# A gated MLP's down projection for the second half of the rows in seven products of quarter matrices per block, with the sums of its weights formed by GpSimd during attention

## The chip, the cores and the metric

The kernel runs on one core of a Trainium2 chip. Five engines work side by side and meet at semaphores: TensorE (PE) multiplies matrices into PSUM, VectorE (DVE) and ScalarE (ACT) work elementwise and read PSUM, GpSimd (POOL) works elementwise between SBUF tiles, and SyncE (SP) issues most of the DMAs; GpSimd issues the others. The metric is the device time of one execution in microseconds, the median of several runs. "PEld" in a profile is the loading of a matmul's stationary operand, which overlaps the matmuls.

## The reference

A transformer block with adaptive layer norm: attention with 32 heads of width 18, then a gated MLP. S is 2048 rows, D is 576, F is 4608.

```python
mod = (_silu(c) @ w_mod).reshape(c.shape[0], 6, 1, -1)
sa, ca, ga, sb, cb, gb = (mod[:, 0], ..., mod[:, 5])
h = _layernorm(x, axis=-1) * (1 + ca) + sa
x = x + ga * _A_ref(h, A_wqkv, A_wo)
h = _layernorm(x, axis=-1) * (1 + cb) + sb
g = jnp.einsum("bsd,df->bsf", h, w_gate)
u = jnp.einsum("bsd,df->bsf", h, w_up)
x = x + gb * jnp.einsum("bsf,fd->bsd", _sigmoid(g) * u, w_down)
```

Everything is float32. The change touches the last line: `_sigmoid(g) * u` times `w_down`, the down projection.

## The kernel before

**Precision.** A float32 operand is split into a high part that the fast matmul format holds (`hi`, `hh`, `wh`) and a low rest (`lo`, `hl`, `wl`). A product is the sum of three matmuls: high x high, high x low, low x high.

**Stages.** Projections of q, k and v come first, then attention (`for u in range(UNITS)`, 32 units of 16 steps), then the MLP. The MLP goes over two halves of 1024 rows (`half` 0 and 1, "first half" and "second half" below), in each over `NB` = 18 blocks of 256 of the F columns. `seq` lists (half, block, k) with the seven `k` in the order of `ORDER` = 1, 6, 2, 7, 5, 4, 3.

**Gate and up projection.** They already use a scheme of seven products of quarters in place of eight (Winograd's form of Strassen's): the operands are cut in two along rows and along columns, and sums of quarters are multiplied. `product(st, k, acc, first)` (L1077) issues product `k` of a block: two accumulators, `v` = 0 and 1 (gate and up), of seven matmuls of 512 columns each. In the second half the sums of weights are loaded from DRAM (`w<-ws`), four products ahead (`LOOK`). VectorE adds the products together into the tiles `u2`, `u3` and `p1` (L1352, L1364, L1369, L1376, L1382), ScalarE takes the sigmoid of the gate's half (`gate`, L1090 and L1092), VectorE multiplies by the up half and ScalarE writes the high part `hh` (`gate_high`, L1098, L1100, L1102), and VectorE writes the low part `hl` (`gate_low`, L1107), called by `flush()`. So one block leaves 256 gated columns for 1024 rows, in four quarters `(f, r)`: `f` is the half of the 256 columns and `r` the half of the rows.

**Down projection.** `down(before, r, ...)` (L1114) multiplies the block before by its 256 rows of `w_down`: `before` 0 and 1 are called behind the products 6 and 7 of the next block. Of each 128 rows of output and each half of the 576 output columns, six matmuls of 288 columns (L1127: two `f`, three terms) accumulate in a PSUM tile `d` of the pool `pd`, which has three buffers, and VectorE adds the tile to `Oa` in SBUF (L1131). `w_down` was scaled by `gb` and split by GpSimd during attention: `down_parts()` loads a block (L849, which waits for a ScalarE instruction of its attention step by `paced`), multiplies, copies and subtracts (L864 to L866), and writes it to the DRAM tensor `wds` (L871). The loop of attention advances this generator every second step from step 72 on and empties it at step `FROM0` = 240, after which the generator `first_rows` uses GpSimd, starting with `load_wo` (L639 to L656). `down_weights(st)` (L1109) loads a block's `wds` in one DMA behind product 5.

**Order.** Within the MLP the order on PE, DVE and ACT is the order in which the program writes the instructions (`manual_schedule`, from `ORDERED` on); in attention it is so for PE alone. The queues of SP and GpSimd are ordered by a scheduler. Each engine takes its instructions strictly in order, so an instruction that waits holds all behind it. At the end of the first half its rows of `Oa` go to the output and `Oa` is filled from `x1d` for the second (L1135, L1137), on GpSimd's queue. The last block's `down` stands alone at the end.

## Time and profile before

| what | us |
|---|---|
| median of 3 runs | 2890.07 (2889.31 to 2890.46) |
| the profiled execution, its own time | 2886.99 |
| span in it, first to last instruction | 2885.2 |
| PE busy | 2833.0 (98%) |
| PEld busy | 1878.1 (65%) |
| DVE busy | 2212.5 (77%) |
| ACT busy | 1563.1 (54%) |
| POOL busy | 680.2 (24%) |
| share of PE in the chain that ended last | 91% |

All stages read from the same execution: attention lies between about 240 and 1590 us, the first half of the MLP between about 1590 and 2235, the second half from there to the end. An engine's busy share is an average over stages with different limits. The 1.8 us between the span and the execution's own time lie outside the first and last instruction.

A row of a timeline gives start, length, engine, line, operation, output tile<-input tiles, and how many instructions were merged; in brackets the idle time before it and what ended it. The length of merged rows runs to the end of the last one, which is longer than the distance between starts, because consecutive instructions overlap.

### The profile page before, as it was taken

What the parts mean: (1) busy time and instruction counts of PE and PEld (TensorE: products, weight loads), DVE (VectorE), ACT (ScalarE), POOL (GpSimd) and SP (SyncE); (2) the same over time, 40 slices, a digit from 0 to 9 for tenths busy, and PEclk for the clock granted to TensorE, in tenths of its full rate; (3) what the DMA queues carried; (4) which work ended last, traced back from release to release, by engine and by line L of the source; (5) the groups of instructions that cost most, each with busy time, mean ns of one, the idle gap of its engine ahead of it and who ended that gap; (6) DMA issues with size and microseconds to landing.
All of it is one profiled execution on the core that took longest, in us unless ns stands there. A gap on an engine that the chain in (4) does not pass through costs nothing.

```text
span 2885.2 us, 46301 instructions
## 1 busy us (share of the span) xinstructions
PE 2833.0 (98%) x17077; PEld 1878.1 (65%) x17077; DVE 2212.5 (77%) x4055; ACT 1563.1 (54%) x2941; POOL 680.2 (24%) x865
## 2 busy tenths in 40 slices
PE   7999999999999999999999999999999999999998
PEld 5974444444444444444443788888888888888888
DVE  7287888898899988999982878888897555555555
ACT  3216899999987778998779322333333111111111
POOL 4124305544313111562102322222221100000000
PEclk9999999999999999999999999999999999999999
DMA  5344113333312111221224866667767844544443
GB/s 170 126 153 137 56 57 135 128 128 125 118 52 77 40 48 32 96 101 51 69 69 138 292 212 227 239 219 269 282 247 288 296 165 167 169 161 161 161 168 123
DMA packets 136387, 429.27 MB, mean 149 GB/s; under 512 B 19100, under 2 KB 55968, under 8 KB 123872
## 3 DMA queue, kind: packets, MB, share of 16 engines
q1 hardware_dynamic: 119664, 344.20, 35.1%
q0 software_dynamic: 16496, 82.10, 8.1%
q8 instruction: 135, 2.21, 0.3%
q14 instruction: 92, 0.75, 0.1%
HBM read 267.77 MB, written 157.95 MB: 148 GB/s over the span
## 4 chain that ended last, share of the span: by engine, by line
PE 91%; DVE 3%; ACT 3%; DMA 1%; issue 1%; POOL 0%; SPq 0%; ACTq 0%; POOLq 0%; DVEq 0%
PE x L1081 27%; PE o L574 17%; PE d L1127 15%; PE s L472 12%; PE s L954 11%; PE s L297 4%; ACT p L958 2%; PE s L711 2%; PE s L348 2%; DVE mx L478 1%; PE s L598 1%; DVE w L1071 0%; DVE Oa L1131 0%; PE d L1266 0%; DMA wm<-in_w_mod_dram 0%
## 5 line engine op out<-in xcount | busy, mean ns | idle before, releaser
L478 DVE TENSOR_REDUCE mx<-s 128x1 f32<-128x512 f32 x1696 | 1076.9, 685 | 117.7 <-PE s L472 100.0
L958 ACT ACTIVATE p<-s 128x512 f32<-128x512 f32 x2048 | 1069.0, 610 | 140.8 <-PE s L472 67.0
L472 PE MATMUL s<-k,q 54*128 54x512 f32 x1920 | 606.0, 450 | 8.2 <-ACT p L958 1.8
L954 PE MATMUL s<-q,k 56*128 56x512 f32 x1920 | 554.5, 425 | 1.1 <-DVE mx L478 0.4
L574 PE MATMUL o<-p,vaug 128*32 128x512 f32 x4096 | 553.1, 605 | 0.4 <-ACT p L958 0.4
L1127 PE MATMUL d<-wd,hh 128*128 128x288 f32 x2304 | 460.8, 295 | 2.4 <-DVE Oa L1131 2.4
L954 PEld LDWEIGHTS s<-q,k 56*128 56x128 f32 x1920 | 264.3, 185 | 290.6 <-DVE mx L478 175.4
L472 PEld LDWEIGHTS s<-k,q 54*128 54x128 f32 x1920 | 272.6, 184 | 250.2 <-ACT p L958 151.4
L1127 PEld LDWEIGHTS d<-wd,hh 128*128 128x128 f32 x2304 | 373.4, 188 | 8.9 <-DVE Oa L1131 3.1
L1131 DVE TENSOR_TENSOR Oa<-Oa,d 128x288 f32<-128x288 f32 x576 | 256.6, 454 | 135.3 <-PE d L1127 129.4
L1081 PE MATMUL x<-k,w 128*128 128x512 f32 x1512 | 356.1, 390 | 2.4 <-ACT w L1062 2.4
L1127 PE MATMUL d<-wd,hl 128*128 128x288 f32 x1152 | 340.3, 295 | 0.0
L1081 PEld LDWEIGHTS x<-k,w 128*128 128x128 f32 x1512 | 281.6, 188 | 58.9 <-ACT w L1062 2.6
L1081 PE MATMUL x<-big,w 128*128 128x512 f32 x1008 | 237.1, 392 | 2.1 <-DVE u L1369 2.1
L1081 PE MATMUL x<-w,w 128*128 128x512 f32 x1008 | 235.9, 390 | 0.0
L1081 PEld LDWEIGHTS x<-big,w 128*128 128x128 f32 x1008 | 190.0, 189 | 42.0 <-DVE u L1369 2.5
L1127 PEld LDWEIGHTS d<-wd,hl 128*128 128x128 f32 x1152 | 216.2, 188 | 0.0
L1081 PEld LDWEIGHTS x<-w,w 128*128 128x128 f32 x1008 | 187.0, 188 | 36.9 <-DVE u L1352 0.3
L574 PEld LDWEIGHTS o<-p,vaug 128*32 128x32 f32 x4096 | 83.3, 108 | 161.6 <-issue 145.3
L1090 ACT ACTIVATE sg<-x 128x512 f32<-128x512 f32 x36 | 21.5, 598 | 300.7 <-PE x L1081 300.7
L1092 ACT ACTIVATE u<-u 128x512 f32<-128x512 f32 x72 | 45.4, 631 | 239.6 <-DVE u L1369 215.0
L1135 POOL DMA_DIRECT2D out_dram<-Oa x16 | 8.7, 542 | 601.3 <-DVE Oa L1131 601.3
(220 smaller groups left out, 2978.6 us busy)
## 6 DMA issues: line engine op xcount, KB each, us to landing
ws<-w SPq DMA_DIRECT2D x126, 640.0 KB
w<-ws SPq DMA_DIRECT2D x126, 640.0 KB
wd<-wds SPq DMA_DIRECT2D x36, 1152.0 KB
k<-kd SPq DMA_DIRECT2D x60, 360.0 KB
wds<-w POOLq DMA_DIRECT2D x18, 1152.0 KB, 4.8
k<-kd SPq DMA_DIRECT2D x60, 180.0 KB
w<-in_B_w_down_dram POOLq DMA_DIRECT2D x18, 576.0 KB, 4.3
q<-qd SPq DMA_DIRECT2D x64, 144.0 KB
```

The costliest lines, as they stand in the source:

```text
L297: nc.tensor.matmul(acc, w, hT[:, t, cols], start=n == 0, stop=n == len(ts_) - 1)
L348: nc.tensor.matmul(acc[:, 0:HALF], hT[:, k, rows], w, start=n == 0, stop=n == len(ts_) - 1,)
L472: nc.tensor.matmul(sp, qs[rows, qt * P : (qt + 1) * P], ks[rows, at * 512 : (at + 1) * 512], start=True, stop=True,)
L478: nc.vector.tensor_reduce(to, sp, axis=AX.X, op=ALU.max)
L574: nc.tensor.matmul(acc[32 * j : 32 * j + 32, :], vaug[:, kt, (2 * p + h) * VW : (2 * p + h) * VW + 32], probs[2 * c + h], start=kt == 0, s ...
L711: nc.tensor.matmul(acc[:, :HALF], a, w, start=i == 0, stop=i == len(ts_) - 1)
L954: nc.tensor.matmul(sT, ks[rows, kcols], qs[rows, c * 512 : (c + 1) * 512], start=True, stop=True)
L958: state["exp"] = nc.scalar.activation(pr, sT, AF.Exp, scale=SCALE)
L1081: nc.tensor.matmul(acc[v], w[:, v, a, :], X[s][:, b, :], start=first and n == 0, stop=n == 6, skip_group_check=not first,)
L1092: nc.scalar.activation(t[:, 0:512], t[:, 0:512], AF.Sigmoid)
L1127: nc.tensor.matmul(acc[:, :HALF], a[:, f, rows], w[:, f, cols], start=n == 0, stop=n == 5)
L1131: nc.vector.tensor_add(Oa[:, t, cols], Oa[:, t, cols], acc[:, :HALF])
```

## The change

In the second half, the down projection of the blocks 0 to 15 (`SEVENS` = 16) is also done in seven products. With A the gated block (quarters a11, a12 for the upper 512 rows, a21, a22 for the lower) and B the block of `w_down` (quarters of 128 rows x 288 columns), the products are those of a11, a12, a22 and the sums s1 = a21 + a22, s2 = s1 - a11, s3 = a11 - a21, S4 = a12 - s2 with quarters of B or sums of them.

- **Weights.** In attention GpSimd forms four sums of quarters per block for 16 blocks, splits them like the rest and writes them to a second DRAM tensor, `wtd`. The generator is advanced in three steps of four instead of one of two. The next block's load is issued later in a block than before.
- **The second half's loop.** For blocks 1 to 16 the loop has a branch of its own: `sevenths(j, b - 1, tiles)` issues product `j` of the block before (`TURNS` says which `j` goes with which `k`) in four tiles of three matmuls of 288 columns, two tiles behind each half `v` of `product`. VectorE adds each tile to `Oa`, or to one of four collecting tiles `G1`, `G5`, `G6`, `G7` in SBUF, which are used by more than one quarter of the output.
- **Sums of A.** `sums_of(before)` forms s1, s2, S4 and s3 on VectorE at product 1, ScalarE writes the high parts (`high`) and VectorE the low parts (`low`) later.
- **Loads.** `load_columns` loads quarters of B and their sums (288 columns each, high and low) one per product on SP's queue, a product after the last use of the quarter that they replace.
- **Joining.** During the products of the last block, `joined(n)` adds the collecting tiles to each other and to `Oa`, in eight VectorE instructions of 4 x 288 columns.

Blocks 16 and 17 keep the old `down`.

```diff
--- before.py
+++ after.py
@@ -54,6 +54,8 @@
+SEVENS = NB - 2
+TURNS = {1: 1, 6: 2, 2: 4, 7: 3, 5: 5, 4: 7, 3: 6}
...
+    wtd = dram.tile([SEVENS, P, 4 * D], F32R, name="wtd")
...
-            for i in range(4):
-                cols = slice(i * HALF, (i + 1) * HALF)
-                nc.gpsimd.tensor_mul(raw[:, cols], raw[:, cols], gb_b[:, i % 2 * HALF : (i % 2 + 1) * HALF])
-                nc.gpsimd.tensor_copy(hi[:, cols], raw[:, cols])
-                nc.gpsimd.tensor_sub(lo[:, cols], raw[:, cols], hi[:, cols].bitcast(F32))
-                if i == 1 and b + 1 < NB:
-                    ahead = load(b + 1)
-                if i < 3:
+            quads = [slice(i * HALF, (i + 1) * HALF) for i in range(4)]
+            b11, b12, b21, b22 = (raw[:, q] for q in quads)
+
+            def split(i):
+                nc.gpsimd.tensor_copy(hi[:, quads[i]], raw[:, quads[i]])
+                nc.gpsimd.tensor_sub(lo[:, quads[i]], raw[:, quads[i]], hi[:, quads[i]].bitcast(F32))
+
+            for i, q in enumerate(quads):
+                nc.gpsimd.tensor_mul(raw[:, q], raw[:, q], gb_b[:, i % 2 * HALF : (i % 2 + 1) * HALF])
+                if i == 2:
                     yield
+            if b < SEVENS:
+                two = [temp([P, 2048], F32R) for _ in range(2)]
+                (t1, t2), (t3, t4) = ([x[:, (2 + i) * HALF : (3 + i) * HALF].bitcast(F32) for i in range(2)] for x in two)
+                nc.gpsimd.tensor_sub(t1, b12, b11)
+                nc.gpsimd.tensor_sub(t3, b22, b12)
+                yield
+                nc.gpsimd.tensor_sub(t2, b22, t1)
+                nc.gpsimd.tensor_sub(t4, t2, b21)
+            if b + 1 < NB:
+                ahead = load(b + 1)
+            yield
+            split(0)
+            split(1)
+            yield
+            split(2)
+            split(3)
             nc.gpsimd.dma_start(wds[b].bitcast(F32), t[:, 0 : 4 * D].bitcast(F32))
             yield
+            if b < SEVENS:
+                for i, x in enumerate(two):
+                    for k in range(2):
+                        to, part = x[:, k * HALF : (k + 1) * HALF], x[:, (2 + k) * HALF : (3 + k) * HALF]
+                        nc.gpsimd.tensor_copy(to, part.bitcast(F32))
+                        nc.gpsimd.tensor_sub(part, part.bitcast(F32), to.bitcast(F32))
+                    nc.gpsimd.dma_start(
+                        wtd[b, :, 2 * D * i : 2 * D * (i + 1)].bitcast(F32), x[:, 0 : 2 * D].bitcast(F32)
+                    )
+                    yield
 
     def last_rows_project():
         for t in range(8, NT):
...
-            if 4 * NT + 8 <= step < FROM0 and step % 2 == 0:
+            if 4 * NT + 8 <= step < FROM0 and step % 4 != 3:
...
-    def product(st, k, acc, first):
+    def product(st, k, acc, first, halves=(0, 1)):
         s, w = ORDER.index(k), st["w", k]
-        for v in range(2):
+        for v in halves:
...
+        st["t", f, r] = t
+        if st["half"] and st["b"] < SEVENS and (f, r) == (0, 1):
+            return None
...
+    late = {}
+
+    def second_half():
+
+        rawst.close()
+        pool = ctx.enter_context(tc.tile_pool(name="late", bufs=1, side="right"))
+        late["G"] = {k: pool.tile([P, 4, HALF], F32, name=f"G{k}") for k in (1, 5, 6, 7)}
+        late["wt"] = pool.tile([P, 2, 2, 2, HALF], F32R, name="wt")
+        late["S4"] = pool.tile([P, 512], F32, name="S4")
+        late["hx"] = pool.tile([P, 3, 512], F32R, name="hx")
+        late["lx"] = pool.tile([P, 3, 512], F32R, name="lx")
+
...
+    def sevenths(j, b, tiles):
+
+        (h, l), w = rows_of(j), columns_of(j)
+        for t in tiles:
+            rows = slice(t * P, (t + 1) * P)
+            acc = pd.tile([P, 512], F32, name="d")[:, 0:HALF]
+            for n, (a, k) in enumerate(((h, 0), (h, 1), (l, 0))):
+                nc.tensor.matmul(acc, a[:, rows], w[:, k, :], start=n == 0, stop=n == 2)
+            if j in late["G"]:
+                to = late["G"][j][:, t, :]
+                if b == 0:
+                    nc.vector.tensor_copy(to, acc)
+                else:
+                    nc.vector.tensor_add(to, to, acc)
+            elif j == 4:
+                to = Oa[:, 4 + t, 0:HALF]
+                nc.vector.tensor_sub(to, to, acc)
+            else:
+                to = Oa[:, t, 0:HALF] if j == 2 else Oa[:, t, HALF:D]
+                nc.vector.tensor_add(to, to, acc)
+
+    def high(j, t):
+        nc.scalar.copy(rows_of(j)[0], t)
+        late["t", j] = t
+
+    def low(j):
+        h, l = rows_of(j)
+        nc.vector.tensor_sub(l, late.pop(("t", j)), h.bitcast(F32))
+
+    def sums_of(st):
+
+        a11, a12, a21, a22 = st["t", 0, 0], st["t", 1, 0], st["t", 0, 1], st["t", 1, 1]
+        s1, s2, s3 = (
+            sums.tile([P, 2, 3, P], F32, name=f"S{k}").rearrange("p v t c -> p (v t c)")[:, 0:512] for k in (1, 2, 3)
+        )
+        nc.vector.tensor_add(s1, a21, a22)
+        nc.vector.tensor_sub(s2, s1, a11)
+        high(5, s1)
+        high(6, s2)
+        yield
+        nc.vector.tensor_sub(late["S4"], a12, s2)
+        nc.vector.tensor_sub(s3, a11, a21)
+        high(3, late["S4"])
+        high(7, s3)
+        yield
+
+    def joined(n):
+
+        G = late["G"]
+        r0, r1 = Oa[:, 0:4, :], Oa[:, 4:8, :]
+        pairs = (
+            (G[6], G[1]), (r0[:, :, 0:HALF], G[1]), (G[7], G[6]), (r0[:, :, HALF:D], G[6]), (r1[:, :, 0:HALF], G[7]),
+            (r1[:, :, HALF:D], G[7]), (r0[:, :, HALF:D], G[5]), (r1[:, :, HALF:D], G[5]),
+        )
+        to, a = pairs[n]
+        nc.vector.tensor_add(to, to, a)
+
...
+        sevens = hf == 1 and 0 < b <= SEVENS
+        if sevens:
+            if at or b > 1:
+                load_columns(b if at else b - 1, TURNS[seq[n - 1][2]])
+            if b == 1 and k in (1, 6, 2, 7):
+                load_columns(0, {1: 3, 6: 5, 2: 7, 7: 6}[k])
+            if k == 1:
+                made = sums_of(before)
+                next(made)
+                st["a"], first = banks(), True
+                acc, to, by = st["a"], None, None
+            elif k == 6:
+                st["b_"], first = banks(), True
+                st["u2"] = ep.tile([P, 1024], F32, name="u2")
+                acc, to, by = st["b_"], st["u2"], st["p1"]
+            elif k == 2:
+                acc, first, to = st["a"], False, None
+                for r in range(2):
+                    st["hh", r], st["hl", r] = late["hh", r], late["hl", r]
+            elif k == 7:
+                st["u3"] = ep.tile([P, 1024], F32, name="u3")
+                acc, first, to, by = st["b_"], False, st["u3"], st["p1"]
+            elif k == 5:
+                st["c"], first = banks(), True
+                acc, to, by = st["c"], st["u3"], st["u3"]
+            elif k == 4:
+                acc, first, to, by = st["b_"], False, st["p1"], st["p1"]
+            else:
+                acc, first, to, by = st["c"], False, st["u2"], st["u2"]
+            f, r = {2: (0, 0), 5: (1, 1), 4: (1, 0), 3: (0, 1)}.get(k, (None, None))
+            for v in range(2):
+                product(st, k, acc, first, (v,))
+                if to is not None:
+                    nc.vector.tensor_add(half(to, v), acc[v], half(by, v))
+                if v == 0 and f is not None:
+                    t = gate(st, to)
+                sevenths(TURNS[k], b - 1, (2 * v, 2 * v + 1))
+                if v == 0:
+                    if k == 1:
+                        next(made)
+                        st["p1"] = ep.tile([P, 1024], F32, name="p1")
+                        nc.scalar.copy(half(st["p1"], 0), acc[0])
+                    elif k == 6:
+                        low(3)
+                    elif k == 2:
+                        low(5)
+                    elif k in (7, 4, 3):
+                        flush()
+                elif k == 1:
+                    nc.scalar.copy(half(st["p1"], 1), acc[1])
+            if f is not None:
+                got = gate_high(st, t, f, r)
+                if got:
+                    behind.append(got)
+            if k in (2, 7):
+                low({2: 6, 7: 7}[k])
+            if k == 3:
+                before = st
+                st["wd"] = late["wd"][:, 0], late["wd"][:, 1]
+            continue
...
+            got = gate_high(st, *kept)
+            if got:
+                behind.append(got)
+        if hf and not b and k in (4, 3):
+            load_columns(0, {4: 2, 3: 4}[k])
+        if hf and b == NB - 1:
+            for i in {1: (0, 1), 2: (2, 3), 5: (4,), 4: (5, 6), 3: (7,)}.get(k, ()):
+                joined(i)
```

Three places show how the change moves instructions. First PE, inside a block of the second half (x: an accumulator of the gate and up projection; k_ and w_: parts of the MLP's input; d: the down projection's PSUM tile; wd, wt: its weights). Before, the products 1 and 6 and the first tile of the `down` behind them:

```order
L1081 MATMUL x<-k_20118,w 128x512 x14
L1081 MATMUL x<-k_20578,w 128x512 x14
L1127 MATMUL d<-wd,hh_31562 128x288 x2
L1127 MATMUL d<-wd,hl_31563 128x288
L1127 MATMUL d<-wd,hh_31562 128x288 x2
L1127 MATMUL d<-wd,hl_31563 128x288
```

and after, the second half of product 2, the two tiles behind it, and the first half of product 7:

```order
L1113 MATMUL x<-w_20984,w 128x512 x7
L1195 MATMUL d<-wt,hh_27565 128x288 x2
L1195 MATMUL d<-wt,hl_27566 128x288
L1195 MATMUL d<-wt,hh_27565 128x288 x2
L1195 MATMUL d<-wt,hl_27566 128x288
L1113 MATMUL x<-w_20986,w 128x512 x7
```

A run of 28 matmuls of 512 columns and then 48 of 288 columns has become an alternation of 7 and 6; a tile `d` now ends after three matmuls instead of six.

Second DVE, at the seam between two of those blocks, product 3 of one (`u_...` is its `u2`) and product 1 and the first part of 6 of the next. Before:

```order
L1382 TENSOR_TENSOR u_31763<-x,u_31763 128x512 x2
L1100 TENSOR_TENSOR u_31763<-u_31763 128x512
L1107 TENSOR_TENSOR hl_31849<-u_31763,hh_31848 128x512
L1352 TENSOR_TENSOR u_32047<-x,p_32026 128x512 x2
L1131 TENSOR_TENSOR Oa<-Oa,d 128x288 x8
```

and after (G_...: collecting tiles; S_...: the sums of A; sg, u and p: the block's gated quarters):

```order
L1508 TENSOR_TENSOR u_32134<-x,u_32134 128x512
L1201 TENSOR_TENSOR G_27448<-G_27448,d 128x288 x2
L1132 TENSOR_TENSOR u_32134<-u_32134 128x512
L1223 TENSOR_TENSOR S_32389<-u_32134,u_32218 128x512
L1224 TENSOR_TENSOR S_32390<-S_32389,sg 128x512
L1201 TENSOR_TENSOR G_27446<-G_27446,d 128x288 x2
L1228 TENSOR_TENSOR S_27451<-p_32109,S_32390 128x512
L1229 TENSOR_TENSOR S_32391<-sg,u_32134 128x512
L1201 TENSOR_TENSOR G_27446<-G_27446,d 128x288 x2
L1508 TENSOR_TENSOR u_32444<-x,p_32419 128x512
L1207 TENSOR_TENSOR Oa<-Oa,d 128x288 x2
```

Between the last gating product (L1132) and the next block's first addition (L1508) there stood one low part (L1107); now there are four sums and four additions of tiles `d`.

Third DVE in the last block, products 4 and 3. Before:

```order
L1376 TENSOR_TENSOR p_32026<-x,p_32026 128x512 x2
L1100 TENSOR_TENSOR p_32026<-p_32026 128x512
L1107 TENSOR_TENSOR hl_32131<-p_32026,hh_32130 128x512
L1382 TENSOR_TENSOR u_32047<-x,u_32047 128x512 x2
L1131 TENSOR_TENSOR Oa<-Oa,d 128x288 x2
L1100 TENSOR_TENSOR u_32047<-u_32047 128x512
L1131 TENSOR_TENSOR Oa<-Oa,d 128x288 x2
```

and after:

```order
L1580 TENSOR_TENSOR p_32713<-x,p_32713 128x512 x2
L1132 TENSOR_TENSOR p_32713<-p_32713 128x512
L1243 TENSOR_TENSOR Oa<-Oa,G_27449 128x4x288
L1243 TENSOR_TENSOR Oa<-Oa,G_27447 128x4x288
L1142 TENSOR_TENSOR hl_27564<-p_32713,hh_27563 128x512
L1586 TENSOR_TENSOR u_32737<-x,u_32737 128x512 x2
L1243 TENSOR_TENSOR Oa<-Oa,G_27447 128x4x288
L1267 TENSOR_TENSOR Oa<-Oa,d 128x288 x2
L1132 TENSOR_TENSOR u_32737<-u_32737 128x512
L1267 TENSOR_TENSOR Oa<-Oa,d 128x288 x2
```

Two joining additions (L1243) now stand in front of the low part that the last `down` reads (L1142), and a third in front of the first addition of that `down` (L1267).

46 lines of the change are left out of this document (40 added, 6 removed).

## The prediction

> **What bounds the kernel now.** I read the page first, then the busy times by stage, then the chain of waits in order of time through the last block.
>
> ```profile
> PE 91%; DVE 3%; ACT 3%; DMA 1%; issue 1%; POOL 0%; SPq 0%; ACTq 0%; POOLq 0%; DVEq 0%
> L1131 DVE TENSOR_TENSOR Oa<-Oa,d 128x288 f32<-128x288 f32 x576 | 256.6, 454 | 135.3 <-PE d L1127 129.4
> 350.00:400.00 50.00, 49.65 (x330) 20.23 (x326) 44.89 (x85) 47.19 (x96) 2.68 (x4) 1.00 0.11 32
> 500.00:550.00 50.00, 49.65 (x331) 20.59 (x332) 44.78 (x85) 47.38 (x95) 21.90 (x36) 1.00 0.34 115
> 2600.00:2650.00 50.00, 50.00 (x282) 44.66 (x281) 27.65 (x49) 7.38 (x13) 0.00 (x0) 1.00 0.51 169
> ```
>
> A row of the stages holds sum, PE, PEld, DVE, ACT and POOL (instructions in brackets), clock, DMA share, GB/s. In the second half (last row) PE is never idle at full clock, DVE is busy 27.65 of 50 us, POOL not at all, and VectorE waits for PE: 129.4 us before its additions of `d`. There a matmul less is its time less, as long as VectorE keeps up. In attention PE, DVE and ACT are all near full; GpSimd has room.
>
> ```profile
> 2835.80 6.36 PE d L1127 x48
> 2842.16 6.36 PE x L1081 x28
> 2848.52 6.36 PE d L1127 x48
> 2854.89 9.53 PE x L1081 x42
> 2864.42 7.97 PE d L1127 x60
> ```
>
> The chain gives the matmuls' true distances, without the overlap that single rows hide: 6.36 / 48 = 0.1325 us for 288 columns and 6.36 / 28 = 0.227 us for 512, and no gap where one kind follows the other. A block is 98 x 0.227 + 96 x 0.1325 = 35.0 us.
>
> **The change part by part.** *Matmuls.* `down` has 2 x 4 x 2 tiles of six, 96 per block; the sevenths 7 x 4 tiles of three, 84. Sixteen blocks save 192 x 0.1325 = **25.4 us**, and a block takes 98 x 0.227 + 84 x 0.1325 = 33.4 us. Switching 28 times instead of four between the two kinds costs nothing by the rows above. [...]
>
> *VectorE in the loop.* It loses nothing and gains, per block, 12 additions of tiles, 4 sums and 3 low parts.
>
> ```profile
> L1100 DVE TENSOR_TENSOR p<-p x36: 676/692/695, 1618.2 to 2862.3; 128x512 f32<-128x512 f32 x36
> 2863.71 0.69 DVE L1107 TENSOR_TENSOR hl<-p,hh 128x512 fp32r<-128x512 f32 x1 [0.69 <-ACT hh L1102]
> 2864.32 1.28 DVE L1382 TENSOR_TENSOR u<-x,u 128x512 f32<-128x512 f32 x2
> ```
>
> With 25 instructions of 512 columns at 0.69 us and 28 of 288 at 0.454, a block needs 30.0 us of its 33.4 (before: 18 and 16, 19.7 of 35.0); the starts 2863.71 and 2864.32 show that independent instructions follow after 0.61, so the true load is lower. In a half of a product (PE: 7 x 0.227 + 6 x 0.1325 = 2.39 us) it has at most one addition of 512, two of 288 and one more of 512: 2.29. The exception is the seam of the second order fence: from the last half of product 3 through the first of product 1 it has six of 512 and four of 288, 5.96 us against 4.77. So it falls 1.2 us behind, more where the gate's multiplication must wait for the addition before it. PE feels that only when a buffer of `d` is wanted again. Laying the rows out with the full 0.69 and 0.454 plus 0.05 for each semaphore, the tightest buffer is free 0.3 us before PE needs it; with 0.61 there is over 1 us. I take **0**; if this cover is gone, PE waits once per block, some 0.5 us, 8 in all, and that is my upper bound.
>
> *Loads.*
>
> ```profile
> w<-ws SPq DMA_DIRECT2D x126, 640.0 KB
> wd<-wds SPq DMA_DIRECT2D x36, 1152.0 KB
> ```
>
> Per block seven loads of 288 KB replace the one of 1152 KB, beside seven of 640, so SP moves 6.65 MB instead of 5.77. By the last stage row, 169 GB/s at a share of 0.51, full use would be near 330 GB/s; 6.65 MB in 33.4 us is 199. A quarter is wanted six products after its load is issued, 29 us. Each of these loads waits only for the product just finished, so the next `w<-ws` behind it in SP's queue is not held: **0**.
>
> *GpSimd in attention.*
>
> ```profile
> 428.62 0.79 POOL L849 DMA_DIRECT2D w<-in_B_w_down_dram  x1 [13.44 <-ACT p L958]
> 563.14 0.71 POOL L849 DMA_DIRECT2D w<-in_B_w_down_dram  x1 [7.05 <-ACT p L958]
> 567.77 1.56 POOL L864 TENSOR_TENSOR w<-w,gb_b 128x288 f32<-128x288 f32 x2 [3.91 <-DMA w<-in_B_w_down_dram]
> 569.28 0.78 POOL L865 CAST w<-w 128x288 fp32r<-128x288 f32 x2
> 575.67 0.59 POOL L871 DMA_DIRECT2D wds<-w  x1 [0.30 <-POOL w L866]
> 774.61 0.59 POOL L871 DMA_DIRECT2D wds<-w  x1 [0.30 <-POOL w L866]
> 849.30 0.61 POOL L639 DMA_DIRECT2D t<-in_A_wo_dram  x1 [34.58 <-ACT p L958]
> 896.10 0.81 POOL L617 TENSOR_TENSOR Oa<-oT,rec 128x144 f32<-128x144 f32 x2 [4.27 <-ACT oT L613]
> L678 PEld LDWEIGHTS s<-ident,Oa x32: 138/140/145, 904.1 to 1075.0; 128*128 128x128 f32 x32
> ```
>
> A block takes 563.14 to 576.26, 13.1 us, with its load's landing. Added are eight two-input instructions of 0.78, four copies of 0.39 and two DMA issues of 0.59: 9.0, with a share of L617 22.6 us. From the first load (step 72) to `load_wo` (step 240) a step lasts (849.30 - 428.62) / 168 = 2.50 us; seven calls in three of four steps are 23.4 us. So GpSimd keeps pace and ends near 428.6 + 122 x 4/3 x 2.50 = 836 instead of 775, before 849. Does a busier GpSimd slow the others? The two stage rows of attention, at 2.68 and 21.90 us of POOL, have the same 85 DVE, 96 and 95 ACT and 330 and 331 PE instructions. **0**, and below nothing is excluded because no work leaves attention.
>
> *The joins.* A join has 4 x 288 = 1152 columns: 0.454 + 864 x (0.692 - 0.454) / 224 = 1.37 us. In the last block they stand between instructions that feed the last `down`.
>
> ```profile
> 2858.90 0.69 DVE L1100 TENSOR_TENSOR u<-u 128x512 f32<-128x512 f32 x1
> 2860.33 0.69 DVE L1107 TENSOR_TENSOR hl<-u,hh 128x512 fp32r<-128x512 f32 x1 [0.74 <-ACT hh L1102]
> 2862.33 0.69 DVE L1100 TENSOR_TENSOR p<-p 128x512 f32<-128x512 f32 x1
> 2864.25 0.42 PE L1127 MATMUL d<-wd,hh 128*128 128x288 f32 x2
> ```
>
> Product 5's join fills VectorE's wait of 0.74 and makes the rest 0.5 us late. The two of product 4 come between the multiplication (2862.33 + 0.5) and the low part that began at 2863.71: it now ends near 2866.7. PE wants it for the sixth matmul of the first tile, at 2864.25 + 5 x 0.1325 = 2864.9: 1.8 us of wait. Then product 3's two additions and the last join delay the first tile's addition to about 2869.6, while PE has its three buffers full at 2868.4: 1.2 more. Product 2's two joins make the `down` behind product 7 wait 0.2. Together **3.2 us**; 0 if I have a position wrong, 5.5 if the last four joins were all exposed.
>
> *The start of the second half.*
>
> ```profile
> 2281.22 0.55 POOL L1137 DMA_DIRECT2D Oa<-x1d  x1 [2.27 <-DMA out_dram<-Oa]
> DMA to landing us min/median/max: 4.1/4.1/4.1
> 2260.00:2270.00 10.00, 10.00 (x48) 8.36 (x47) 5.98 (x10) 2.51 (x4) 1.62 (x3) 1.00 0.91 301
> ```
>
> The last tile of `Oa` lands at 2285.3. Before, it was added to behind product 7; now product 2 of block 1 does it, near 2284.6, and eight loads of 288 KB in place of one of 1152, 1.2 MB more, come into a stretch with a DMA share of 0.91 at 301 GB/s: up to 4 us later. VectorE may stand 1 to 4 us, half of which its buffers hide: **1 us**, bounds 0 and 3.
>
> The sum: 25.4 - 3.2 - 1.0 = 21.2 us less. Span 2864.0, profiled execution 2865.8; the median of the runs shown was 3.1 above the profiled execution, so 2890.07 - 21.2 = **2868.9 us**.
>
> **The rivals.**
>
> *VectorE becomes the bound* (slower). For: 53 instructions per block in strict order, 90% by durations. It decides from 35.0 us per block. If a tile's addition cost as much as one of 512 columns (the nearest dearer row), 53 x 0.69 = 36.6 us, 16 x (36.6 - 35.0) = 26 us slower, with the joins 2919. Against: the 0.454 has 576 instances between 0.440 and 0.456. [...] Chance 0.07.
>
> *GpSimd falls behind in attention.* A block of x us makes `load_wo` 16 (x - 23.4) late; the 13 us before 849, the 4.3 before 896.10 and some 7 until PE reads `Oa` at 904.1 absorb 24, so it decides from 24.9. At 26 it gives back 18 us: 2887; at 28, 50: 2919. For: 22.6 is close, and more instructions now wait on GpSimd's own results. Chance 0.05, about half on each side of no change.
>
> *The steady loop leaks at the seams*: 8 to 15 us back, 2876 to 2884. Chance 0.11. *Joins and start are hidden*: 2864.6. Chance 0.08. Anything that I do not see, slower: 0.03. That the matmuls are not saved is excluded by the order of PE: 192 fewer.
>
> **How the numbers follow.** The forecast has 0.66, with a range of its own of 2865 to 2876. The range to 2863 and 2883 takes in the hidden joins and the leaks, by the upper bounds 25.4 - 5.5 - 3 - 8 = 9 less, 2881. About 0.2%, 5.8 us, can be told from no change: faster 0.66 + 0.08 + 0.11 = 0.85, same 0.03, slower 0.12.
>
> **What would show it.** Blocks of the second half 33.4 us apart; PE 50 of 50 there with DVE near 40 to 44; PE rows of 7 and 6 without gaps; POOL done with `wtd` before 849 and the same instruction counts in attention; waits of PE for VectorE of about 3 us in the last 20. Wrong: PE waiting for VectorE in every block, or `load_wo` late.

## The result, and the profile after

The changed kernel took 2885.48 us (median of 11 runs, 2879.64 to 2894.37), the kernel before 2891.87 (11 runs, 2888.45 to 2893.95): a ratio of 0.9982, 95% interval 0.997 to 0.9993. That is 0.18% faster, hardly to be told from no change, and outside the predicted 2863 to 2883. Here and below a ratio rests on all runs of both kernels, and can differ by up to 0.0009 from that of the medians. The runs of the changed kernel spread over 15 us, those of the kernel before over 5.5.

The profiled execution of the changed kernel is the fastest of its eleven, 2879.64. Its page begins so, and the chain that ended last no longer is almost all PE:

```profile
span 2877.8 us, 46834 instructions
PE 83%; POOL 6%; DVE 4%; issue 3%; ACT 2%; DMA 1%; SPq 0%; POOLq 0%; ACTq 0%; DVEq 0%
```

GpSimd had 0% of that chain before and has 6% now. To place the difference I cut the span at three events: the first exponential of attention, the first product of the MLP, and the last product. A row of a line's instructions gives shortest, median and longest duration in ns, and the starts of the first and of the last. The exponentials, the products with operand `k` (the first product) and with `big` (the last), before:

```profile
L958 ACT ACTIVATE p<-s x2048: 570/603/716, 238.5 to 1585.3; 128x512 f32<-128x512 f32 x187
L1081 PE MATMUL x<-k,w x1512: 387/389/481, 1590.8 to 2857.7; 128*128 128x512 f32 x189
L1081 PE MATMUL x<-big,w x1008: 387/389/632, 1606.9 to 2864.0; 128*128 128x512 f32 x168
```

and after:

```profile
L989 ACT ACTIVATE p<-s x2048: 570/603/716, 242.8 to 1600.7; 128x512 f32<-128x512 f32 x187
L1113 PE MATMUL x<-k,w x1512: 387/389/632, 1606.2 to 2850.6; 128*128 128x512 f32 x189
L1113 PE MATMUL x<-big,w x1008: 387/389/504, 1623.7 to 2856.9; 128*128 128x512 f32 x168
```

Attention, from the first exponential to the first product, went from 1352.3 to 1363.4 us; the MLP, from the first to the last product, from 1273.2 to 1250.7; the tail from 21.2 to 20.9. The MLP won 22.5 us, attention lost 11.1, and 4.3 were lost ahead of attention. (The tail ends with the last output stores.)

The steady loop of the second half is as predicted. First its row of the stages (sum, PE, PEld, DVE, ACT, POOL, clock, DMA share, GB/s), then three steps of the chain, with no gap between the kinds of matmul:

```profile
2600.00:2650.00 50.00, 50.00 (x273) 43.91 (x272) 39.48 (x80) 10.32 (x17) 0.00 (x0) 1.00 0.59 193
```

```profile
2598.05 0.80 PE d L1195 x6
2598.85 1.62 PE x L1113 x7
2600.47 0.80 PE d L1195 x6
```

The loss in attention sits in few places. Ten-microsecond rows of the changed kernel:

```profile
690.00:700.00 10.00, 7.60 (x43) 2.74 (x42) 5.91 (x11) 6.67 (x14) 10.00 (x18) 0.83 0.48 147
700.00:710.00 10.00, 10.00 (x72) 4.26 (x68) 8.59 (x17) 9.09 (x18) 6.56 (x11) 1.00 0.73 271
810.00:820.00 10.00, 6.55 (x41) 2.96 (x41) 7.10 (x14) 5.57 (x11) 9.98 (x18) 0.96 0.40 122
820.00:830.00 10.00, 9.32 (x50) 3.52 (x51) 4.81 (x10) 7.71 (x16) 5.33 (x10) 0.70 0.90 326
```

An undisturbed row (the second) has 72 matmuls; the others have 43, 41 and 50. PE is idle for 2.4 and 3.5 us, and behind each gap it runs at a lower granted clock (0.57 from 696 to 700, 0.50 from 820 to 826). Over all 135 such rows from 240 to 1590 us, PE's missing busy time rose from 13.1 to 20.8 us, and the clock that was not granted (10 us times what the clock lacks of 1.00, summed) from 2.1 to 8.5 us. A part of this is only the first row, 240 to 250, as attention began 4.3 us later. The three disturbed rows alone make 6.5 us of idle time and 5.1 us of clock, together about the 11.1 us that attention lost.

The waits of 430 to 900 us (engine, line, what for; total, times, longest) and the timeline around 690 say who was late. "POOL w L873 <- DMA w" is GpSimd waiting for a load of `w_down` to land, that is, for its data to arrive:

```profile
POOL w L873 <- DMA w<-in_B_w_down_dram: 106.9, 18, 11.8
POOL w L852 <- ACT p L989: 13.4, 1, 13.4
ACT oT L591 <- POOL Oa L620: 6.8, 2, 4.3
PE o L577 <- ACT oT L591: 6.5, 2, 4.1
```

```profile
652.38 0.73 POOL L852 DMA_DIRECT2D w<-in_B_w_down_dram  x1
664.90 3.09 POOL L873 TENSOR_TENSOR w<-w,gb_b 128x288 f32<-128x288 f32 x4 [11.79 <-DMA w<-in_B_w_down_dram]
688.13 3.10 POOL L873 TENSOR_TENSOR w<-w,gb_b 128x288 f32<-128x288 f32 x4 [5.18 <-DMA w<-in_B_w_down_dram]
693.83 0.81 POOL L620 TENSOR_TENSOR Oa<-oT,rec 128x144 f32<-128x144 f32 x2
694.67 0.59 ACT L591 COPY oT<-o 128x512 f32<-128x512 f32 x1 [2.57 <-POOL Oa L620]
695.31 1.07 PE L577 MATMUL o<-p,vaug 128*32 128x512 f32 x8 [2.40 <-ACT oT L591]
```

Line 620 (617 before) is attention's own work on GpSimd: it takes the last pair of heads out of `oT`. It stands in GpSimd's queue among the instructions of `down_parts`, here behind a multiplication that waited 5.18 us for its load, after one that had waited 11.79. `oT` has one buffer, so ScalarE may not copy the next pair's accumulator `o` into it before line 620 has read it; `o` is not free until that copy, and TensorE waits to write it. GpSimd's pacing wait (line 852 on ScalarE: a load may be issued only once the exponential of its step is done), 106.1 us in 17 waits before, is left in one wait of 13.4 us, ahead of the first load. Between the blocks GpSimd has no reserve left.

### The profile page after: what moved, and what is told of

Read it like the earlier page. It is cut to its first block, busy times and chain, and to the rows that moved or that the text cites. A ratio compares the mean times of both kernels' runs of the same rounds, so it can differ in the third digit from the quotient of the medians.

```text
span 2877.8 us, 46834 instructions
## 1 busy us (share of the span) xinstructions
PE 2820.3 (98%) x16885; PEld 1855.6 (64%) x16885; DVE 2336.0 (81%) x4367; ACT 1591.6 (55%) x2989; POOL 821.3 (29%) x1089
## 4 chain that ended last, share of the span: by engine, by line
PE 83%; POOL 6%; DVE 4%; issue 3%; ACT 2%; DMA 1%; SPq 0%; POOLq 0%; ACTq 0%; DVEq 0%
PE x L1113 26%; PE o L577 14%; PE s L475 10%; PE s L985 10%; PE d L1263 8%; PE d L1195 6%; PE s L300 4%; PE s L714 2%; PE s L351 2%; ACT p L989 2%; POOL w L870 1%; POOL t L899 1%; DVE mx L481 1%; POOL w L873 1%; PE s L601 1%
## 5 line engine op out<-in xcount | busy, mean ns | idle before, releaser
L1113 PE MATMUL x<-k,w 128*128 128x512 f32 x1512 | 369.7, 392 | 2.4 <-ACT w L1094 2.4
L1263 PE MATMUL d<-wd,hh 128*128 128x288 f32 x1280 | 256.7, 295 | 3.8 <-DVE Oa L1267 3.7
L1113 PE MATMUL x<-w,w 128*128 128x512 f32 x1008 | 245.1, 391 | 0.0
L1113 PE MATMUL x<-big,w 128*128 128x512 f32 x1008 | 244.3, 391 | 0.0
L1263 PEld LDWEIGHTS d<-wd,hh 128*128 128x128 f32 x1280 | 207.2, 188 | 8.7 <-DVE Oa L1267 5.1
L1263 PE MATMUL d<-wd,hl 128*128 128x288 f32 x640 | 189.1, 295 | 1.6 <-DVE hl L1142 1.6
L1267 DVE TENSOR_TENSOR Oa<-Oa,d 128x288 f32<-128x288 f32 x320 | 139.9, 453 | 55.6 <-PE d L1263 51.7
L1094 ACT CAST w<-S 128x768 fp32r<-128x768 f32 x72 | 60.1, 835 | 134.9 <-POOL S L1072 133.4
```

The lines of the kernel that those rows point to most:

```text
L1094: nc.scalar.copy(w[:, :, 0:3, :], src)
L1113: nc.tensor.matmul(acc[v], w[:, v, a, :], X[s][:, b, :], start=first and n == 0, stop=n == 6, skip_group_check=not first,)
L1263: nc.tensor.matmul(acc[:, :HALF], a[:, f, rows], w[:, f, cols], start=n == 0, stop=n == 5)
L1267: nc.vector.tensor_add(Oa[:, t, cols], Oa[:, t, cols], acc[:, :HALF])
```

## The experiments

Each kernel of an experiment ran beside the kernel before on the same chip. The stretches of the profiles, cut as above, are each of one execution:

| kernel | ratio to before (95%) | first exp at | attention | first to last product | tail |
|---|---|---|---|---|---|
| before | | 238.5 | 1352.3 | 1273.2 | 21.2 |
| changed | 0.9982 (0.997 to 0.9993) | 242.8 | 1363.4 | 1250.7 | 20.9 |
| after_again | 0.9974 (0.9963 to 0.9985) | 242.2 | 1362.2 | 1254.6 | 20.9 |
| second_alone | 0.9948 (0.9936 to 0.9961) | 239.9 | 1355.5 | 1251.2 | 24.1 |
| attention_alone | 1.0035 (1.0023 to 1.0048) | 241.0 | 1365.2 | 1273.0 | 17.9 |
| sums_no_stores | 1.0005 (0.9996 to 1.0014) | 243.4 | 1354.5 | 1272.5 | 21.2 |
| before_two | 1.0000 (0.9991 to 1.0009) | 242.4 | 1351.8 | 1273.0 | 21.2 |
| oT_two | 0.9951 (0.9939 to 0.9964) | 243.0 | 1362.2 | 1251.1 | 20.9 |
| oT_rec_two | 0.9932 (0.9921 to 0.9944) | 243.0 | 1352.2 | 1253.1 | 20.9 |
| load_on_SP | 0.9959 (0.9945 to 0.9972) | 243.9 | 1359.4 | 1252.0 | 24.0 |
| both_mended | 0.9960 (0.9948 to 0.9971) | 242.2 | 1359.1 | 1250.4 | 23.9 |
| joins_sooner | 0.9950 (0.9938 to 0.9961) | 239.0 | 1355.2 | 1252.8 | 22.3 |
| rec_two_joins | 0.9946 (0.9930 to 0.9962) | 243.3 | 1362.0 | 1252.1 | 19.4 |
| stores_on_SP | 1.0149 (1.0133 to 1.0164) | 243.0 | 1417.7 | 1260.4 | 22.8 |
| late_rows | 0.9926 (0.9913 to 0.9938) | 243.5 | 1352.5 | 1251.3 | 19.3 |

**The two halves of the change apart.** second_alone has the old `down_parts` and its old pace. It leaves the sums out: the second half reads plain quarters where the sums should be, with the same matmuls and the same number of bytes. Besides the old `down_parts`, its edit is this:

```diff
-            kept = wtd[b].rearrange("p (a l i d) -> p a l i d", a=2, l=2, i=2)
+            kept = wds[b].rearrange("p (a l i d) -> p a l i d", a=2, l=2, i=2)
-            if 4 * NT + 8 <= step < FROM0 and step % 4 != 3:
+            if 4 * NT + 8 <= step < FROM0 and step % 2 == 0:
```

> Leaves out the quarter sums of w_down: attention does GpSimd's old work, and the second half reads plain quarters in their place (same bytes from memory, same instructions). Theory (the gain of the second half is there in full, the loss sits in attention): about 21 us under before, ratio 0.992 to 0.993; first matmul of the first half of the MLP at about 1591 us as before, clock as before. Rival (the second half itself costs more in some executions): a spread as wide as the change's 15 us and a ratio near 0.998. Rival (the shift of 4.3 us ahead of attention is part of the change's second half, by its buffers): the first exp of attention at about 243 us instead of 238.5.

attention_alone keeps the new `down_parts`, while the second half's loop is the old one (`USED` = 0 in place of `SEVENS` there; one line of several):

```diff
-        sevens = hf == 1 and 0 < b <= SEVENS
+        sevens = hf == 1 and 0 < b <= USED
```

> Sums and their stores are made, but the second half works as before and doesn't read them. Theory: 11 to 16 us over before, ratio 1.004 to 1.0055, all of it between 450 and 900 us, with two or three idle stretches of TensorE of 2 to 4 us behind oT, each with a granted clock of 0.7 to 0.9 in the 10 us after it. Rival (GpSimd's extra work takes memory or engine time evenly): no idle stretch, but exps in each 50 us fewer by one or two. Rival (the loss needs the second half): ratio 1.000.

Measured: 2872.5 against 2889.64 for the first, 2900.37 for the second. The MLP's gain stands alone, 22.0 us between first and last product, and attention's loss stands alone, 12.9 us, with idle stretches at 690 (6.86 us busy of 10) and 810 (4.62). By their ratios the two halves, 0.52% faster and 0.35% slower, make 0.17% faster together; the whole change is 0.18% faster. Both ratios missed their ranges. That of attention_alone, 1.0035, is a little under 1.004. That of second_alone is 0.9948 where 0.992 to 0.993 was expected: its attention, though the work is the old one, was 3.2 us longer than in the profile of before, and its tail 2.9. One cause in attention is a drop of the clock that the section on the hardware shows; the tail's is open. The first exponential came between 238.5 and 243.9 us in all profiles, at 242.4 in before_two, which has no part of the change: the 4.3 us ahead of attention are a spread of executions.

**The changed kernel again.**

> The changed kernel once more, beside the others on one chip. Theory (GpSimd late, ACT then TensorE held at oT): the same two idle stretches of TensorE near 690 and 810 us, TensorE's busy time short of the 240 to 1590 us stretch by 18 to 22 us, a clock dip behind each; ratio 0.997 to 0.9995. Rival (the stretches of the first profile were a chance of that one execution): they are gone or elsewhere, and the time is near 2874 us.

2881.7 against 2889.7. The stretch at 690 us returned (7.34 us busy of 10, then a clock of 0.55 from 700 on); the one at 810 did not, and a smaller one came at 530, where ScalarE does not wait for GpSimd (TensorE waits 1.0 us for a load of `q`). So one of the two expected stretches came, ScalarE waited for `oT` once, 2.8 us, and attention still lost 9.9 us. The place varies; the loss was nearly the same.

**Whose wait it is.** oT_two gives every second pair of heads of the first half of attention a buffer of its own, and oT_rec_two doubles the small tile `rec` as well, which line 620 reads too:

```diff
-            oT = epool.tile([P, 512], F32, name="oT")
+            other = p % 2 and half == 0 and 2 < p
+            oT = bgp.tile([P, 512], F32, name="oU") if other else epool.tile([P, 512], F32, name="oT")
-        rec = epool.tile([P, 4, 4], F32, name="rec")
+        rec = epool.tile([P, 4, 4], F32, name="rec", bufs=2)
```

> Every second pair of heads of the first half of attention puts oT into a buffer of its own, so that ACT's copy doesn't wait for GpSimd's last use. Theory: GpSimd stays as late as in the change (last wds store at about 855 us, landing waits near 105 us), but ACT's wait on GpSimd for oT and the idle stretches of TensorE are gone: about 10 us under the change, ratio 0.994 to 0.995. Rival (GpSimd's lateness itself passes on to w_o and the first rows): ratio stays at 0.998 with new waits behind 865 us.

> As oT_two, and the small tile rec has two buffers as well, since with oT doubled VectorE waited 7.6 us for GpSimd at rec and TensorE 6.8 us behind it. Theory: no wait of TensorE, ACT or VectorE on GpSimd between 430 and 900 us, no 10 us stretch there under 8.5 us of TensorE, though GpSimd's landing waits stay above 100 us; 2 to 5 us under oT_two, ratio 0.993 to 0.9945. Rival (GpSimd's lateness shows at its next user): a new wait of 5 us or more on GpSimd, ratio as oT_two (0.995).

oT_two took 2874.36 against 2889.64. Its profiled execution is the slowest of its five, 2879.04. In it ScalarE's wait for `oT` on GpSimd was gone, and the next tile read by line 620 (621 in these kernels) took its place:

```profile
POOL w L874 <- DMA w<-in_B_w_down_dram: 113.9, 18, 12.4
DVE rec L606 <- POOL Oa L621: 7.6, 1, 7.6
PE s L986 <- ACT oT L617: 6.8, 1, 6.8
```

VectorE stood 7.6 us at `rec`, and TensorE 6.8 behind it. With `rec` doubled too, oT_rec_two took 2870.65 against 2889.7 (2868.87 to 2871.53), and its attention 1352.2 us, what it took before. GpSimd is as late as ever, or later:

```profile
POOL w L874 <- DMA w<-in_B_w_down_dram: 117.3, 18, 13.3
L893 POOL DMA_DIRECT2D wds<-w x18: 578/578/608, 449.5 to 865.8; - x18
```

So in this execution lateness by itself cost nothing; in the changed kernel the single buffers passed it on. The control is the same edit in the kernel before:

> The kernel before with oT and rec in two buffers and nothing else. Theory: before has no wait of ACT on GpSimd for oT, so the buffers are worth nothing there: ratio 0.9995 to 1.0005. Rival (the buffers are a gain of their own, and the change lost less in attention than it seems): ratio 0.996 to 0.998.

2890.16 against 2889.69, a ratio of 1.0000: the buffers are no gain of their own.

**Why GpSimd is late.** sums_no_stores is attention_alone without the two stores of the sums:

```diff
-                    nc.gpsimd.dma_start(
-                        wtd[b, :, 2 * D * i : 2 * D * (i + 1)].bitcast(F32), x[:, 0 : 2 * D].bitcast(F32)
-                    )
```

> attention_alone without the two stores of the quarter sums: GpSimd makes the sums, splits them, and nothing carries them out (the second half doesn't read them). Theory (the stores delay the next block's load, and that delay is what makes GpSimd late): landing waits fall from 107.8 us to under 75, GpSimd's block to about 21 us of work and then the pace, no wait of ACT on oT, ratio 0.9995 to 1.0005. Rival (the GpSimd work alone is too long): landing waits fall, but the wait of ACT on oT and the idle stretches stay, ratio 1.002 to 1.004. Rival (the load lands late without the stores as well): landing waits near 100 us.

2892.09 against 2890.53, where attention_alone had lost 10.7 us: without the stores the loss is gone. The mechanism in the expectation was only a part of it. The waits for the load fell only from 107.8 to 94.2 us:

```profile
POOL w L874 <- DMA w<-in_B_w_down_dram: 94.2, 18, 11.0
POOL w L853 <- ACT p L987: 28.2, 7, 13.4
L893 POOL DMA_DIRECT2D wds<-w x18: 593/593/611, 449.7 to 834.3; - x18
```

The larger part of the gain is the time that GpSimd itself no longer spends on issuing these stores. A row of the changed kernel shows one, with the wait for GpSimd's own last result ahead of it:

```profile
651.79 0.60 POOL L900 DMA_DIRECT2D wtd<-t  x1 [0.30 <-POOL t L899]
```

Thirty-two issues of about 0.57 us and sixteen waits of 0.30 make 23 us; with the 13.6 of landing, less 14.7 more of pacing (28.2 in place of 13.5), 22 us are removed; from the first store of `wds` to the last it is 384.6 us instead of 406.5 (449.7 to 834.3, and 447.5 to 854.0).

The 94.2 us that remain are not the same wait 18 times. In the changed kernel 14 of the 18 waits for the load last 3.6 to 6.5 us and four last 8.6 to 11.8. Without the stores of the sums 14 last 2.9 to 4.7 us, 3.7 in the mean, as before the change, and four still last 10.6 to 11.0. What the four have in common is attention's own loads of q and k, eight on SP's queue every 40 us, 1.5 MB together. Here are the first and the last of one group in the changed kernel, on both sides of the load issued at 652.38 that was waited for 11.79 us:

```profile
648.28 0.79 SPq L440 DMA_DIRECT2D q<-qd  x1
653.86 0.98 SPq L448 DMA_DIRECT2D k<-kd  x1
```

In these two profiles all eight long waits are for a load issued during such a group or within 2 us of its end, and no load issued at another time was waited for that long. In the kernel before, the pacing kept the loads clear of the groups. Every second load was issued just ahead of one, here by 0.36 us; this one was waited for 3.49 us, and no wait for a load in that kernel exceeds 5.7:

```profile
642.77 0.71 POOL L849 DMA_DIRECT2D w<-in_B_w_down_dram  x1 [7.07 <-ACT p L958]
643.13 0.78 SPq L437 DMA_DIRECT2D q<-qd  x1
```

So the stores of the sums lengthen the usual wait by about 1.1 us, some 15 us in all, and the long waits come with the loads of q and k. That rests on the times alone; no run moves those loads.

Two kernels moved DMAs to SP's queue, one the load and one the stores:

```diff
-            paced(nc.gpsimd.dma_start(
+            paced(nc.sync.dma_start(
                 t[:, 2 * D : 4 * D].bitcast(F32).rearrange("p (t d) -> p t d", d=D),
```

> The load of w_down's next block goes into SP's queue and no longer stands behind the three stores in GpSimd's. Theory: GpSimd's waits for that load fall from 106.9 us to under 50, its block to about 19 us of work ahead of the pace, no wait of ACT on GpSimd for oT, first matmul of the MLP at about 1595 us, time 2868 to 2874 (ratio about 0.993). Rival (stores and loads share the transport, whatever the queue): landing waits stay near 100 us and the time at 0.998. Rival (SP's queue then holds q, k and mrows loads back behind this load): new waits of TensorE or VectorE on q or mrows, and a time above the change's.

```diff
-            nc.gpsimd.dma_start(wds[b].bitcast(F32), t[:, 0 : 4 * D].bitcast(F32))
+            nc.sync.dma_start(wds[b].bitcast(F32), t[:, 0 : 4 * D].bitcast(F32))
-                    nc.gpsimd.dma_start(
+                    nc.sync.dma_start(
                         wtd[b, :, 2 * D * i : 2 * D * (i + 1)].bitcast(F32), x[:, 0 : 2 * D].bitcast(F32)
```

> The changed kernel (single buffers) with the three stores of a block in SP's queue instead of GpSimd's; the load stays in GpSimd's. Theory (the load lands late because it stands behind the stores in one queue): GpSimd's landing waits fall from 106.9 us to about the 64 to 67 us of before, the block from 24.6 to about 21 us, the wait of ACT on oT is gone; ratio 0.993 to 0.995. Rival (they share the transport): the waits stay over 95 us. Rival (SP's queue, full of stores that wait for GpSimd, holds q and mrows back): TensorE or VectorE waits on DMA, ratio over 0.998.

load_on_SP took 2878.55 against 2889.64, slower than the expected 2868 to 2874. GpSimd was on time (last `wds` store at 834.5) and ScalarE's wait for `oT` gone; 79.9 us of waiting for the load remained instead of under 50, a part of it pace, as SP's queue held the load 153.2 us for the step's exponential. But a stretch of 6.94 us busy of 10 came at 1430 us, far behind `down_parts`, where TensorE waits for the row tile of `project_o`. One near there is in the profiles of all three kernels with the load on SP and in no other; why is open. stores_on_SP failed by its second rival, 2935.22 against 2889.69. SP takes its queue in order and stood 201.6 us at stores whose data GpSimd had not made, ahead of the loads that TensorE needed:

```profile
SPq L892 <- POOL w L870: 201.6, 18, 29.0
POOL w L873 <- DMA w<-in_B_w_down_dram: 97.6, 18, 11.3
PE s L985 <- DMA q<-mrows: 43.2, 12, 10.3
```

Its second row is worth keeping: with no store in its own queue the load was still waited for 97.6 us. So standing behind the stores in one queue is not, or not alone, what delays it.

**Combinations.**

> oT and rec in two buffers and the load of w_down on SP's queue. Theory: each alone already takes the idle stretches away, so the two together are no faster than the better one, ratio 0.993 to 0.995, and equal to second_alone (0.9948) within its interval. Rival (each takes away a part of its own): ratio under 0.9925.

2878.4 against 2889.7, a ratio of 0.9960, slower than oT_rec_two alone and outside the expected range, with the stretch at 1430 us again: here the load is better left in GpSimd's queue.

```diff
-            for i in {1: (0, 1), 2: (2, 3), 5: (4,), 4: (5, 6), 3: (7,)}.get(k, ()):
+            for i in {1: (0, 1, 2), 2: (3, 4, 5), 5: (6, 7)}.get(k, ()):
```

> both_mended with the eight joins at products 1, 2 and 5 of the last block instead of 1, 2, 5, 4 and 3. Theory: the waits of TensorE on VectorE in the last two products (1.6 us for the low part, 0.8 us for a d buffer) go, and nothing else moves: 2 to 2.4 us less between the last product's end and the end of the span. Rival (joins in product 5 hold the gate and the high part back): a wait of TensorE on VectorE for hh or hl of 1 us or more.

> oT_rec_two with the joins sooner, the load left in GpSimd's queue. Theory: the idle stretch at 1430 us, which came with the load on SP's queue, isn't there, and the tail loses 2 to 3 us: 2867 to 2869 against 2889.7, ratio 0.992 to 0.993, the best of all. Rival (the tail is set by the last stores, not by VectorE): ratio as oT_rec_two, 0.9932.

joins_sooner took 2875.5, within both_mended's interval; its tail was 1.6 us shorter where 2 to 2.4 were expected. rec_two_joins took 2874.89 against 2889.69, and its six runs reach from 2864.88 to 2880.34: neither the 2867 to 2869 nor the best of all. Its profile shows attention 9.7 us longer than before, at the place that the prediction had feared. GpSimd waited 12.64 us for one load, finished `wds` at 873.40, and its preparation of `w_o` came too late for `project_o`:

```profile
873.40 0.58 POOL L893 DMA_DIRECT2D wds<-w  x1 [0.30 <-POOL w L871]
DVE t L688 <- POOL we L657: 7.1, 1, 7.1
PE s L475 <- DVE t L688: 5.9, 1, 5.9
```

late_rows puts six more steps of attention between that preparation and its first use:

```diff
         weights.extend((wo_h, wo_l, we))
-        for _ in range(4):
+        for _ in range(10):
             yield
```

> rec_two_joins with the first row tile's projection six steps (about 15 us) further behind w_o's preparation, since in rec_two_joins' profile GpSimd ended the weights at 873 us and the last part of w_o held VectorE 7.1 us and TensorE 5.9 us at 910 us. Theory (what is left of GpSimd's lateness shows there, in some executions): no wait behind w_o's tiles, no idle stretch at 910 us, the spread of the runs narrows from 15 us to about 5; 2867 to 2870, ratio 0.992 to 0.993. Rival (the spread comes from elsewhere, the clock dips ahead of 250 and at 1600 us): spread and median as in rec_two_joins, 0.9946.

2868.39 against 2890.53 (2867.86 to 2874.27), ratio 0.9926, the lowest of all, though its interval and that of oT_rec_two overlap. It is 22.1 us under its kernel before, where the change was 6.4 under its own. In its profile nothing waits at `w_o`, `oT` or `rec`, with GpSimd's last `wds` store at 858.1. That the spread narrowed from 15.5 to 6.4 us rests on five runs. The sooner joins bring little of it: the tail is 1.6 us shorter than in oT_rec_two, but TensorE waits 1.3 us for VectorE at 2834 instead.

## Why the prediction was wrong, step by step

- **Matmuls, VectorE, loads of the second half: right in kind, the saving put too high.** The same instruction in two successive blocks, after the change (L1223, the first sum of A) and before it (L1352, the first addition of product 1):

```profile
2353.03 0.69 DVE L1223 TENSOR_TENSOR S<-u,u 128x512 f32<-128x512 f32 x1
2386.62 0.69 DVE L1223 TENSOR_TENSOR S<-u,u 128x512 f32<-128x512 f32 x1
2344.87 0.69 DVE L1352 TENSOR_TENSOR u<-x,p 128x512 f32<-128x512 f32 x1 [1.49 <-PE x L1081]
2379.83 0.69 DVE L1352 TENSOR_TENSOR u<-x,p 128x512 f32<-128x512 f32 x1 [1.49 <-PE x L1081]
```

  That is 33.59 us for a block instead of 34.96, so 1.37 are saved and not the 1.59 of the sum: 21.9 us in 16 blocks in place of 25.4. The new block takes 0.2 us more than its sum of 33.4. The prediction put its 28 changes between the two kinds of matmul at nothing; 0.008 us for each would make the difference, but that they are the cause is not shown. Between first and last product 22.5 us came in this kernel, 19 to 23 in the others with the new loop, stores_on_SP aside (12.8; why is open). PE is busy 50.00 of 50 us. VectorE is busy 39.48 of 50 us, 26.4 per block of 33.4, under the 30.0 by durations and far from the bound.
- **Joins: right, a little too dear.** Predicted 3.2 us, of which 1.8 for the low part and 1.2 for a buffer of `d`; the waits of TensorE were these two, 2.4 us together:

```profile
2859.54 0.40 PE L1263 MATMUL d<-wd,hl 128*128 128x288 f32 x1 [1.59 <-DVE hl L1142]
2862.37 0.53 PE L1263 MATMUL d<-wd,hh 128*128 128x288 f32 x2 [0.84 <-DVE Oa L1267]
```

- **Start of the second half**: predicted 1 us. VectorE waited 1.8 us for the last tile of `Oa`, and TensorE waited for nothing there: 0.

```profile
DVE Oa L1204 <- DMA Oa<-x1d: 1.8, 1, 1.8
```

- **"GpSimd in attention", 0 us: wrong**, by two steps. The first is a size. The block was put at 22.6 us with "its load's landing" as before, 3.9 us. It was read from loads that stood behind a pacing wait, which kept them clear of other transfers. The changed kernel has no pacing left, the load follows the stores at once, some loads fall among those of q and k, and the landing wait is 106.9 / 18 = 5.9 us in the mean. The sixteenth store of `wds` gives the block:

```profile
L892 POOL DMA_DIRECT2D wds<-w x18: 581/581/611, 449.5 to 855.4; - x18
818.58 0.58 POOL L892 DMA_DIRECT2D wds<-w  x1
```

  (818.58 - 449.5) / 15 = 24.6 us, the 22.6 and 2.0 more, against a pace of 23.4; and 836 + 16 x 1.2 = 855, which is where the first row ends.
- The second step is the one that failed as reasoning: "So GpSimd keeps pace", and, in the rival, that a late GpSimd first costs anything at `load_wo`, "so it decides from 24.9". The prediction asked only when GpSimd would finish, not what else stands in its queue. Line 617 was in the quoted rows, as slack; in fact it is a consumer with a deadline in every pair of heads, and its tiles `oT` and `rec` have one buffer each. So it decides somewhere between the pace, 23.4, and 24.6: sums_no_stores and load_on_SP, which keep pace and end by 834.5, have no wait of ScalarE on GpSimd for `oT`, and the changed kernel with 24.6 has it. By the prediction's own rule 24.6 was still free, and for `load_wo` it was: nothing waits for `w_o` in the changed kernel's profile. oT_rec_two, which breaks just this coupling, gives 0.9932, and late_rows, which also covers `w_o`, 0.9926. The forecast was 2868.9 / 2890.07 = 0.9927; that late_rows meets it is in part luck, as the matmuls saved 3.5 us less than forecast and late_rows also has other joins.
- "The same instruction counts in attention" as a sign was well chosen: 43, 41 and 50 matmuls for 72 showed the error at once. That the clock would fall behind the stalls, by 5.1 us not granted in the three disturbed rows, was in no term of the sum.

## What to carry to other kernels

Work that is added to an engine "with room" has to be laid beside the deadlines of everything else in that engine's queue, and each small tile with one buffer is such a deadline: here two of them turned lateness of GpSimd, busy for 29% of the span, into stalls of TensorE, busy for 98% (6.5 us behind `oT` in the changed kernel, 6.8 behind `rec` in oT_two). A wait taken from a profile holds only while its neighbours do: the load that was issued after a pacing wait was waited for 67.3 / 18 = 3.7 us in the mean, and 5.9 once that wait was used up, with the four longest, 8.6 to 11.8 us, for loads issued during those of q and k or within 2 us of their end. Two kilobytes per partition for a second buffer were worth more here (0.9932 in oT_rec_two) than either move of DMAs to SP's queue (0.9959 and 1.0149).

## What the hardware showed

A stall of TensorE cost more than its length in some of these profiles, and only its length in others. At the same place of attention, with the same instructions, VectorE holds TensorE for 1.6 us in every profile (1.3 in late_rows). Behind it the clock fell in five of the fifteen profiles, to 0.69 to 0.88 in the mean of a ten-microsecond row; in the other ten it stayed at 1.00. In second_alone it fell (two-microsecond rows, PE first, then the clock as the third number from the end):

```profile
1102.00:1104.00 2.00, 0.38 (x4) 0.12 (x2) 0.94 (x3) 1.67 (x4) 1.03 (x1) 0.95 0.00 0
1104.00:1106.00 2.00, 2.00 (x10) 0.38 (x10) 2.00 (x5) 0.00 (x0) 0.00 (x0) 0.50 0.00 0
1108.00:1110.00 2.00, 2.00 (x12) 0.29 (x10) 1.54 (x8) 1.43 (x3) 0.00 (x0) 0.50 0.00 0
```

and in oT_rec_two it did not:

```profile
1106.00:1108.00 2.00, 1.28 (x10) 0.34 (x10) 2.00 (x5) 0.52 (x2) 0.00 (x0) 1.00 0.00 0
1108.00:1110.00 2.00, 2.00 (x18) 0.67 (x14) 2.00 (x6) 1.26 (x3) 0.00 (x0) 1.00 0.00 0
```

Ten matmuls in 2 us against eighteen, for some 7 us. Summed over the two-microsecond rows from 1102 to 1112, the clock not granted is 3.4 us, so the 1.6 us stall costs either 1.6 us or some 3 more. Idle times of 1.6 us (second_alone) and 2.4 us (the changed kernel at 692 to 696) were followed by a clock of 0.50 and 0.57; what decides whether it falls was not shown. I take these falls to be one part of why runs of one kernel spread; that is a guess, which no run tried by itself.
